# New places in the order of an attention and of the seam between two layers, with one small scratch moved out of PSUM

## The chip, the cores and the metric

The kernel runs on one core of a Trainium2 chip. Its time is the device time of one launch, in microseconds (us); lower is better. The engines are named as in the profile: PE (TensorE, matmuls; PEld is its weight load), DVE (VectorE), ACT (ScalarE), POOL (GpSimd) and SP, whose queue issues nearly all DMAs.

## What is computed

An attention over 2 x 8 heads (768 positions, 64 wide) in which a query sees only keys of the same hash bucket, and two layers behind it (1536 tokens, 512 wide, 2048 inside), cut here to its core:

```python
q_bits = (einsum('bhsd,dk->bhsk', q, proj) > 0)      # 6 bits give a bucket; k likewise
scores = where(q_bucket == k_bucket, q @ k.T / 8, -1e9)
x = softmax(scores) @ v                               # heads laid side by side: 1536 x 512
h = x @ w_in;  x = (P(h) / (Q(h) + 1e-6)) @ w_out     # layer 1, P cubic, Q with |h| and h*h
h = x @ w_in2; out = (h - tanh(h)) @ w_out2           # layer 2
```

## The kernel before

Heads go one after the other, h = 0 to 15, and each head in six steps j of 128 queries. A step multiplies scores into PSUM (`scores`, tiles st, L930), ACT takes the exponential (e, L933), ACT and DVE round it to 16 bits (eh, L942, L944), POOL takes the rest (el, L953), and PE multiplies both with V (`attend`, L985 to L988, with V's own high and low half in VB). Ahead of the scores of a head, six maxima are needed: PE makes the products a second time (`smax`, tiles sm, L810), DVE reduces each to a column of mx (L814), `put_max` turns the columns into rows with a transpose on PE (sbank<-ident,mx, L825), DVE negates them (mr, L831), and a DMA lays them into row 76 of TBq. The bucket bits come from `bits` on PE (L785), and DVE writes them into TBk (L795), from where a DMA takes 12 rows to TBq (L798). The operands of both products reach their places by DMAs within SBUF: `place` issues TBk and TBq (L768, L769), and `out_of place` four DMAs into TA (L775).

V is loaded for two heads at a time (`load_v`, tile vraw, L850). DVE takes the maximum of its magnitudes (vm, L854), a DMA lays the 128 pairs into one row (vrow, L859), the function `back` in `vall` reduces that row to two numbers and makes a power of two of each (L865 to L869), and a further DMA spreads them (vsc, L873). ACT then scales V into VB (L894), and `vmean_of` sums V on PE (sbank<-VB, L911), which ACT and DVE make into VM (L917, L918).

PSUM has three places for st, sm and bits tiles, which go round in the order in which the tiles are made, so that a new tile waits until the tile three before it was read. One further bank, sbank, is shared: the transposes of `put_max`, the sums of `vmean_of` and, on partition 64, the two numbers of `back` all lie in it, and the framework makes PE and DVE wait for each other there. `fill` puts matmuls without use on PE (pvw<-ones, L966).

All engines run in program order, and that order is written out by a list of tasks. Each task has a place on a line counted in steps of heads; the table MOVE shifts single tasks, and the tasks are emitted sorted by place:

```python
def on(place, fn, *args):
    tasks.append((place + MOVE.get(move_name(fn, args), 0), len(tasks), fn, args))
```

FILL lists places and counts of `fill`. After the attention a second list does the same with NUDGE, in microseconds of a plan. Between the layers, layer 2 works with sums and differences of blocks: `t_sum` (L1348) makes them on DVE, `x_hi` (ACT, L1359) and `x_lo` (DVE or POOL, L1365) split them, `product` multiplies (L1391), `u1`, `u2`, `u3` add products (`u2` is L1407), `g_lo` (POOL, L1470) gives the low half of the activation, and `y2_mm` (L1486) multiplies it.

Of the kernel before, what the change touches and what calls it, by code (L numbers as in the profile page):

```python
# [10 lines left out]
F32, F32R, F16, BF16, I32 = DT.float32, DT.float32r, DT.float16, DT.bfloat16, DT.int32  # L11
# [5 lines left out]
B, H, S, D = 2, 8, 768, 64  # L17
# [5 lines left out]
SH = S // 2  # L23
# [12 lines left out]
EH_ACT_LAST = (768, 0, 768, 384, 768, 768)  # L36
EL_DVE_LAST = (640, 0, 0, 384, 128, 768)

FILL = ((199.95, 71), (91.54, 25), (-29.26, 33), (-6.1, 72), (-0.79, 4), (-23.35, 19), (8.78, 3), (-23.45, 5), (1.45, 8))

VLO_POOL = (0, 1)

# [104 lines left out]
T_LAST = {'norm': 9.69, 'x': 10.12, 'x_out': 10.83}  # L147

NUDGE = {'stage_e 10 1': 1.68,
 't_sum 0 5 1 3': 1.0571,  # L150
 'rest2 2 1': -1.5624,
 'y_out 9 0': -0.62,
 't_sum 0 2 0 1': 2.09,
# [43 lines left out]
 'y2_mm 0 2': -1.047,  # L197
 'x_lo 1 6 1': -2.4416,
 'x_hi 1 6 1': -1.6436,
 'u3 1 1': 0.4716,  # L200
 'x_lo 0 3 1': 0.8634,
 'g_sub 0 a': 1.5846,
 'g_hi 0 a': 0.9366,
# [34 lines left out]
 'x_hi 0 6 0': 1.0934,  # L238
 'x_lo 0 6 0': 0.4954,
 'x_hi 0 5 1': 0.6058,  # L240
 'x_lo 0 5 1': 0.0078,
 'join2 3 1': -0.1334,
 'x_lo 0 4 0': 1.003,
 'g_lo 0 a': 0.3386,
# [5 lines left out]
 'x_hi 1 0 0': -0.2366,  # L250
 'g_lo 0 d': -1.1453,
 'g_hi 0 d': -0.6889,
 'g_sub 0 d': -0.0409}
MOVE = {'fill 25': 8.577,
 'attend 2 1': -0.953,
 'smax 15 0': -0.153,
# [14 lines left out]
 'vlo 10': 0.153,  # L271
 'smax 1 3': -0.091,
 'scale 1 1': -2.1579,
 'smax 0 2': -1.278,
 'out_of e (13, 2)': -0.263,
 'load_qk 2': 3.2764,
 'vall 0': 12.2053,
 'place 1': -0.1816,
 'round_e 8 5': 0.213,
 'out_of vmean 15': 0.073,  # L280
 'out_of place 1': 0.9139,
# [5 lines left out]
 'fill 19': -1.743,  # L287
 'out_of max (0, 2)': 0.006,
 'out_of max (13, 5)': 0.393,
 'load_qk 1': 0.1764,  # L290
 'attend 8 2': -0.953,
 'load_v 0': -1.2766,
 'attend 4 2': -0.953,
# [18 lines left out]
 'normalize 15': -0.377,  # L312
 'vhi 8': -0.1387,
 'attend 12 1': -0.883,
 'vhi 2': 0.553,
 'vlo 1': 0.073,
 'out_of place 3': -0.2893,
 'scores 13 0': 0.07,
 'round_e 15 5': 0.3926,
 'vmax 0': 10.6854,  # L320
 'scores 9 1': -0.055,
 'out_of max (0, 0)': 1.02,
 'smax 0 0': 1.318,
 'out_of bits 0': 10.916,
 'out_of e (15, 1)': -0.473,
 'scores 15 1': -0.055,
 'round_e 14 4': 0.006,
 'out_of e (14, 4)': -0.01,
 'load_v 1': 2.2916,
 'put_max 15': 0.633,  # L330
 'out_of put 15': 0.625,
 'out_of max (2, 5)': -0.7062,
 'smax 2 5': -0.4082,
 'out_of e (9, 2)': -0.263,
 'attend 13 0': -0.2423,
 'halves 0 1': 0.753,
# [7 lines left out]
 'out_of e (15, 0)': 0.8687,  # L344
 'round_e 15 0': 0.3407,
 'scale 0 1': 1.277,
 'out_of max (15, 4)': -1.2373,
 'smax 15 4': -0.9393,
 'scores 15 0': 0.948,
 'put_max 1': 0.203,  # L350
 'out_of put 1': 0.155,
# [7 lines left out]
 'out_of vmean 0': 0.403,  # L359
 'vhi 12': -0.023,  # L360
 'place 0': -0.568,
 'split_hi 0': -0.27,
 'smax 1 4': -0.153,
 'out_of e (13, 5)': -0.473,
 'scores 13 5': -0.055,
 'rest_e 15 4': 2.093,
 'vmean_of 1': 0.703,
 'out_of vmean 1': 0.553,
 'bits 0': 11.964,
 'smax 0 1': 0.024,  # L370
 'join 1 1': -1.01,
 'round_e 14 5': 1.0,
 'rest_e 14 5': 0.592,
 'attend 0 3': 0.193,
 'attend 14 1': -0.008,
 'scores 15 5': 0.413,
 'scores 7 0': 0.073,
 'round_e 0 2': 0.3044,
 'scale 3 1': -0.383,
 'attend 0 4': -0.103,  # L380
 'halves 2 0': 0.203,
 'scores 1 3': -0.093,
 'halves 2 1': 0.4539,
 'round_e 15 1': -0.003}
J0 = 2
YSQ = (0.9, 4, 3.5)
GC = dict(sub=0.7, hi=1.35, lo=1.95)
# [43 lines left out]
def tile_fn(ctx: ExitStack, tc: tile.TileContext, kq, v, proj, w1i, w1o, a_, b_, w2i, w2o, out):  # L431
# [236 lines left out]
    with ExitStack() as actx:  # L668
        actx.enter_context(tc.manual_schedule(engines={getattr(nc, e).engine for e in ORDERED}))
        ap = actx.enter_context(tc.tile_pool(name="ap", bufs=1))  # L670
# [4 lines left out]
        sbank = sgl.tile([P, 512], F32, name="sbank")  # L675
# [181 lines left out]
        def vall(pr):  # L857
            row = ap.tile([1, 2 * P], F32, name=f"vrow{pr}", tag="vrow", bufs=1)
            nc.sync.dma_start(row.rearrange("o (p h) -> o p h", h=2), vmx.pop(pr))  # L859
            sc = ap.tile([1, 2], F32, name=f"vs1{pr}", tag="vs1", bufs=2)  # L860

            def back():
                o = SH + D + 2 * (pr % 2)
                x = sbank[64:65, o:o + 2]
                nc.vector.tensor_reduce(x, row.rearrange("o (p h) -> o h p", h=2), axis=AX.X, op=ALU.max)  # L865
                xi = x.bitcast(I32)
                nc.vector.tensor_scalar(xi, xi, 0x7F800000, None, op0=ALU.bitwise_and)
                nc.vector.tensor_scalar(x, x, 2.0 ** -87, 2.0 ** -12, op0=ALU.max, op1=ALU.mult)
                nc.vector.reciprocal(sc, x)  # L869

            def again():
                vs = ap.tile([P, 2], F32, name=f"vsc{pr}", tag="vsc", bufs=3)
                nc.sync.dma_start(vs, sc.unsqueeze(1).to_broadcast([1, P, 2]))  # L873
                for j in range(2):
                    vsc[2 * pr + j] = vs[:, j:j + 1]

            outs["vback", pr], outs["vagain", pr] = back, again
# [161 lines left out]
        def on(place, fn, *args):  # L1039
            tasks.append((place + MOVE.get(move_name(fn, args), 0), len(tasks), fn, args))  # L1040
# [48 lines left out]
        for u in range(NE):  # L1089
            for fi in range(FG):  # L1090
                t = end + TT["h0"] + TT["slot"] * (4 * u + fi)
                on(t, h_mm, u, fi)
                for n, f in zip("abcde", (stage_a, stage_b, stage_c, stage_d, stage_e)):
                    on(t + TT[n], f, u, fi)
        for t, n in FILL:
            on(t, fill, n)
# [27 lines left out]
        for _, _, fn, args in sorted(tasks, key=lambda x: x[:2]):  # L1124
            name = fn.__name__
# [555 lines left out]
```

## Time and profile before

| | |
|---|---|
| median of 3 runs | 750.57 us (748.86 to 751.51) |
| profiled execution | 748.52 us, of which the span from first to last instruction is 746.8 us |
| busy in the span | PE 729.5 us (98%), DVE 616.5 (83%), ACT 551.8 (74%), POOL 538.4 (72%) |
| mean granted clock of TensorE | 0.993 of full speed |

Busy shares are means over stages. Since PE is busy for 98% of the span, what can be won without less work lies in the few places where PE waits and in stretches at the lower of its two clocks (0.5 in the profile is 1.2 GHz, 1.0 is 2.4 GHz). An interval in brackets in a timeline is the idle time of an engine ahead of that row, and the name behind the arrow is what ended it.

### The profile page before, as it was taken

To read this page: it belongs to the slowest core of one execution; us is meant where nothing else is said; L and a number is where in the kernel's file an instruction comes from. 1 tells how busy PE (TensorE), PEld (TensorE's weight loads), DVE (VectorE), ACT (ScalarE), POOL (GpSimd) and SP (SyncE) were. 2 spreads that over 40 slices of the span, in tenths; PEclk is the share of its full clock that TensorE was granted. 3 is DMA by queue.
4 is the path that set the end of the run, shared out by engine and by line. 5 is a ranking of instruction groups with operands and counts; after the bars stand their busy time and mean duration, and the time that the engine had idled before them with its cause. 6 is when DMAs were issued, how large, how long until landed. Compare 5 with 4: busy or idle time off the path is not lost.

```text
span 746.8 us, 14449 instructions
## 1 busy us (share of the span) xinstructions
PE 729.5 (98%) x5406; PEld 598.1 (80%) x5406; DVE 616.5 (83%) x1034; ACT 551.8 (74%) x979; POOL 538.4 (72%) x459
## 2 busy tenths in 40 slices
PE   8899999999999999999999999999999999999997
PEld 6788888888888888888888888887887676767664
DVE  7689998999968987899899999989666867778765
ACT  1688889988998787766776677688576768677652
POOL 2679898998998897777787789959646366364531
PEclk8999999999999999999999999999999999999999
DMA  7665546565420321212112212101030220311003
GB/s 197 170 163 141 151 115 173 163 150 166 124 86 30 113 85 57 70 61 69 56 57 86 75 39 70 44 2 56 29 114 32 83 85 29 113 57 57 29 29 140
DMA packets 43373, 66.56 MB, mean 89 GB/s; under 512 B 6164, under 2 KB 29812, under 8 KB 43304
## 3 DMA queue, kind: packets, MB, share of 16 engines
q1 hardware_dynamic: 43160, 65.52, 29.8%
q8 instruction: 42, 0.69, 0.4%
q14 instruction: 27, 0.22, 0.1%
q10 hardware_dynamic: 144, 0.13, 0.1%
HBM read 43.00 MB, written 3.15 MB: 62 GB/s over the span
## 4 chain that ended last, share of the span: by engine, by line
PE 74%; DVE 14%; ACT 4%; DMA 3%; POOL 2%; issue 2%; SPq 0%; POOLq 0%; ACTq 0%; DVEq 0%
PE y L1486 16%; PE h L609 16%; PE y L1179 16%; PE h2b L1391 6%; DVE mx L814 4%; PE st L930 4%; PE h2e L1391 4%; PE h2a L1391 4%; PE sm L810 2%; DVE TBk L795 1%; DVE eh L944 1%; POOL x L1365 1%; ACT e L933 1%; PE bits L785 1%; PE pv L985 1%
## 5 line engine op out<-in xcount | busy, mean ns | idle before, releaser
L953 POOL TENSOR_TENSOR el<-e,eh 128x768 f16<-128x768 f32 (+2 forms) x95 | 151.4, 1613 | 22.5 <-DVE eh L944 10.0
L1486 PE MATMUL y<-wS,g 128*128 128x512 f16 (+1 forms) x438 | 102.8, 378 | 0.0
L933 ACT ACTIVATE e<-st,lnk 128x768 f32<-128x768 f32 x96 | 86.1, 898 | 19.0 <-PE st L930 16.9
L814 DVE TENSOR_REDUCE mx<-sm 128x1 f32<-128x768 f32 x96 | 90.0, 950 | 9.5 <-PE sm L810 8.6
L1470 POOL TENSOR_TENSOR g<-tmp,g 128x384 f16<-128x384 f32 x48 | 44.0, 917 | 67.0 <-ACT g L1465 55.4
L665 POOL TENSOR_TENSOR G<-vec,G 128x512 fp32r<-128x512 f32 x44 | 57.2, 1306 | 26.0 <-ACT G L660 25.9
L1486 PEld LDWEIGHTS <-g 128*128 128x128 f16 x438 | 38.5, 98 | 45.6 <-issue 6.3
L1179 PE MATMUL y<-G,wO 128*128 128x512 f32 x288 | 67.1, 391 | 0.0
L1509 DVE SCALAR_TENSOR_TENSOR ya<-y,few,ya 128x512 f32<-128x512 f32 (+1 forms) x73 | 54.0, 741 | 15.0 <-PE y L1486 14.1
L1179 PE MATMUL y<-G,wE 128*128 128x512 f32 x288 | 66.3, 390 | 0.0
L609 PE MATMUL h<-x,wO 128*128 128x512 f32 x288 | 66.3, 390 | 0.0
L1179 PEld LDWEIGHTS y<-G,wE 128*128 128x128 f32 x288 | 54.1, 188 | 11.2
L609 PEld LDWEIGHTS h<-x,wO 128*128 128x128 f32 x288 | 54.1, 188 | 11.2
L1179 PEld LDWEIGHTS y<-G,wO 128*128 128x128 f32 x288 | 53.9, 188 | 11.3 <-POOL G L665 0.3
L942 ACT CAST eh<-e 128x384 f16<-128x384 f32 (+2 forms) x95 | 60.9, 642 | 1.7
L985 PEld LDWEIGHTS <-eh 128*128 128x128 f16 x576 | 53.1, 97 | 10.0 <-issue 9.9
L1391 PE MATMUL h2b<-x,wE 128*128 128x384 f32 x288 | 60.3, 344 | 0.8 <-ACT x L1359 0.8
L985 PE MATMUL pv<-VB,eh 128*128 128x65 f16 x540 | 57.8, 194 | 0.0
L988 PE MATMUL pv<-VB,el 128*128 128x65 f16 x540 | 57.0, 192 | 0.8 <-POOL el L953 0.8
L986 PE MATMUL pv<-VB,eh 128*128 128x64 f16 x540 | 57.4, 195 | 0.0
L930 PE MATMUL st<-TA 128*128 128x384 f32 x192 | 56.4, 375 | 0.5 <-DVE mx L814 0.3
L810 PE MATMUL sm<-TBk,TBq 76*128 76x384 f32 x192 | 52.2, 357 | 3.2 <-DVE TBq L792 2.1
(202 smaller groups left out, 2039.0 us busy)
## 6 DMA issues: line engine op xcount, KB each, us to landing
raw<-in_w1i_dram SPq DMA_DIRECT2D x16, 512.0 KB
raw<-in_w1o_dram SPq DMA_DIRECT2D x16, 512.0 KB
raw<-in_w2i_dram SPq DMA_DIRECT2D x16, 512.0 KB
raw<-in_w2o_dram SPq DMA_DIRECT2D x16, 512.0 KB
kq<-in_kq_dram SPq DMA_DIRECT2D x16, 384.0 KB
TA<-A SPq DMA_DIRECT2D x32, 192.0 KB
TA<-Bl SPq DMA_DIRECT2D x32, 192.0 KB
vraw<-in_v_dram SPq DMA_DIRECT2D x8, 384.0 KB
```

The costliest lines, as they stand in the source:

```text
L609: nc.tensor.matmul(ps, l[:, dc], r, start=(n == 0), stop=(n == 11))
L810: nc.tensor.matmul(ps[:, n], TBq[h][0:76, j * P:(j + 1) * P], TBk[h][0:76, n * SH:(n + 1) * SH], start=True, stop=True)
L814: d = nc.vector.tensor_reduce(mx[h][:, j:j + 1], ps, axis=AX.XY, op=ALU.max)
L930: nc.tensor.matmul(ps[:, n], l[h][0:k, j * P:(j + 1) * P], q[h][0:k, n * SH:(n + 1) * SH], start=(k == P), stop=(k < P))
L933: outs["e", (h, j)] = lambda: nc.scalar.activation(halved(e), ps, AF.Exp, scale=1.0 / math.sqrt(D), bias=lnk)
L942: nc.scalar.copy(t[:, 0:r], e[:, 0:r])
L953: nc.gpsimd.tensor_sub(l[:, r:NK], e[:, r:NK], eh[h, j][:, r:NK])
L985: nc.tensor.matmul(out(t), a[:, t], vb[:, j, 0:PW], start=False, stop=False, skip_group_check=True)
L986: nc.tensor.matmul(out(t)[:, 0:D], a[:, t], vb[:, j, PW:PW + D], start=False, stop=False, skip_group_check=True)
L1179: nc.tensor.matmul(ps, l[:, o], r, start=(n == 0), stop=(n == 11))
L1391: nc.tensor.matmul(banks[n, k], w_in(j, l)[:, o:o + P], x[:, r, dt], start=new and z == 0, stop=z == 5, skip_group_check=not new)
L1486: nc.tensor.matmul(ps[:, c], g[:, l, o], r[:, c], start=(z == 0), stop=(z == 5))
```

## The change

One function changes: the two numbers in `back` lie in a tile of their own in SBUF (vx, two buffers) and no longer in sbank. Everything else is numbers of three tables: FILL, MOVE (about 50 entries changed or added) and NUDGE (4). Where a shift is small it changes nothing; the core of what the diff says is:

```diff
-FILL = ((199.95, 71), (91.54, 25), (-29.26, 33), (-6.1, 72), (-0.79, 4), (-23.35, 19), (8.78, 3), (-23.45, 5), (1.45, 8))
+FILL = ((199.95, 71), (91.54, 25), (-29.26, 52), (-6.1, 72), (-23.35, 19), (6.47, 1), (-11.01, 3))
...
- 't_sum 0 5 1 3': 1.0571,
+ 't_sum 0 5 1 3': -1.4768,
...
- 'load_qk 1': 0.1764,
+ 'load_qk 1': -1.4262,
...
- 'load_v 1': 2.2916,
+ 'load_v 1': 2.2339,
...
             def back():
-                o = SH + D + 2 * (pr % 2)
-                x = sbank[64:65, o:o + 2]
+                x = ap.tile([1, 2], F32, name=f"vx{pr}", tag="vx", bufs=2)
                 nc.vector.tensor_reduce(x, row.rearrange("o (p h) -> o h p", h=2), axis=AX.X, op=ALU.max)
                 xi = x.bitcast(I32)
                 nc.vector.tensor_scalar(xi, xi, 0x7F800000, None, op0=ALU.bitwise_and)
```

The fill counts in the order of the program: 57 become 71 at the start; 3 come new between the maxima of head 0; 76 become 72 ahead of st of head 0, step 0; 8 behind its step 1 go; 3 behind the scores of head 1, step 2 become 1 ahead of those of step 1.

SP's queue at the opening. Names are tiles with running numbers; kq is the load of a head's K and Q, A the rounded K and Q of a head. Before:

```order
L713 DMA kq_109<-in_kq_dram 128x768
L719 DMA praw_108<-in_proj_dram 128x6
L850 DMA vraw_186<-in_v_dram 128x6x128
L768 DMA TBk_192<-A_188 64x768
L769 DMA TBq_193<-A_188 64x768
L713 DMA kq_196<-in_kq_dram 128x768
L775 DMA TA_191<-A_188 64x768 x2
L775 DMA TA_191<-Bl_189 64x768 x2
L768 DMA TBk_232<-A_218 64x768
L769 DMA TBq_233<-A_218 64x768
L859 DMA vrow_259<-vm_236 1x128x2
L713 DMA kq_272<-in_kq_dram 128x768
```

After the change:

```order
L739 DMA kq_109<-in_kq_dram 128x768
L745 DMA praw_108<-in_proj_dram 128x6
L876 DMA vraw_205<-in_v_dram 128x6x128
L739 DMA kq_207<-in_kq_dram 128x768
L794 DMA TBk_214<-A_209 64x768
L795 DMA TBq_215<-A_209 64x768
L801 DMA TA_213<-A_209 64x768 x2
L801 DMA TA_213<-Bl_210 64x768 x2
L739 DMA kq_268<-in_kq_dram 128x768
L885 DMA vrow_270<-vm_245 1x128x2
L794 DMA TBk_279<-A_237 64x768
L795 DMA TBq_280<-A_237 64x768
```

The load of head 1 stands ahead of the first `place`, and the load of head 2 and the small row vrow stand ahead of the second `place`.

SP's queue some 20 us later, around the load of the second piece of V (vraw, for heads 2 and 3). Before:

```order
L713 DMA kq_385<-in_kq_dram 128x768
L768 DMA TBk_388<-A_373 64x768
L769 DMA TBq_389<-A_373 64x768
L775 DMA TA_387<-A_373 64x768 x2
L775 DMA TA_387<-Bl_374 64x768 x2
L798 DMA TBq_389<-TBk_388 12x768
L850 DMA vraw_447<-in_v_dram 128x6x128
L713 DMA kq_463<-in_kq_dram 128x768
L768 DMA TBk_517<-A_486 64x768
L769 DMA TBq_518<-A_486 64x768
```

After the change:

```order
L739 DMA kq_403<-in_kq_dram 128x768
L794 DMA TBk_406<-A_391 64x768
L795 DMA TBq_407<-A_391 64x768
L876 DMA vraw_455<-in_v_dram 128x6x128
L801 DMA TA_405<-A_391 64x768 x2
L801 DMA TA_405<-Bl_392 64x768 x2
L824 DMA TBq_407<-TBk_406 12x768
L794 DMA TBk_473<-A_465 64x768
L795 DMA TBq_474<-A_465 64x768
L739 DMA kq_477<-in_kq_dram 128x768
```

The load of V stands five DMAs earlier (four into TA and the 12 rows of bits), and the load of head 4 two later.

PE around the transposes and the sum of V of head 1 (st are scores of head 0, sm products for the maxima of head 2). Before:

```order
L810 MATMUL sm_0_557<-TBk_388,TBq_389 128x384 x2
L930 MATMUL st_4_569<-TA_191 128x384 x2
L930 MATMUL st_4_569<-TBq_193,TBk_192 128x384 x2
L825 MATMUL sbank<-ident,mx_407 6x128
L810 MATMUL sm_1_582<-TBk_388,TBq_389 128x384 x2
L911 LDWEIGHTS ones_84
L911 MATMUL sbank<-VB_137,ones_84 128x64
```

After the change:

```order
L955 MATMUL st_4_563<-TA_213 128x384 x2
L955 MATMUL st_4_563<-TBq_215,TBk_214 128x384 x2
L836 MATMUL sm_0_569<-TBk_406,TBq_407 128x384 x2
L851 MATMUL sbank<-ident,mx_417 6x128
L955 MATMUL st_5_589<-TA_213 128x384 x2
L955 MATMUL st_5_589<-TBq_215,TBk_214 128x384 x2
L836 MATMUL sm_1_594<-TBk_406,TBq_407 128x384 x2
L936 LDWEIGHTS ones_84
L936 MATMUL sbank<-VB_137,ones_84 128x64
```

The scores of step 5 stand ahead of the sum of V and no longer behind it, and the product for the first maximum of head 2 stands behind the scores of step 4.

On ACT and POOL, rounding head 3's K and Q (A, Bl) stands one step earlier. Elsewhere in the attention single tasks change places: st of heads 7 and 8, step 0, stand one `attend` later, the sum of V of head 7 stands behind the next scores, and `put_max` of head 15 one `attend` earlier. Between the layers, one `t_sum` stands three rows earlier on DVE, and `u2` of the first block now stands between two `x_lo` instead of behind both; ACT and POOL keep their order there.

## Rows read from the trace of the kernel before

**Rows 1.** Timeline of PE, 24 to 36 us: start, us, engine, line, operation, [idle before, releaser].

```profile
24.42 0.52 PE L930 MATMUL st<-TA 128*128 128x384 f32 x2
...
25.13 0.60 PE L966 MATMUL pvw<-ones 128*128 128x122 f16 x8
25.63 1.26 PE L810 MATMUL sm<-TBk,TBq 76*128 76x384 f32 x4
...
34.80 0.80 PE L911 MATMUL sbank<-VB,ones 128*128 128x64 f16 x12 [2.31 <-DVE mr L831]
35.41 0.99 PE L930 MATMUL st<-TA 128*128 128x384 f32 x2
```

**Rows 2.** Timeline of DVE in the same stretch, same columns.

```profile
24.62 0.96 DVE L814 TENSOR_REDUCE mx<-sm 128x1 f32<-128x768 f32 x1
...
30.56 0.95 DVE L814 TENSOR_REDUCE mx<-sm 128x1 f32<-128x768 f32 x1
33.60 0.95 DVE L854 TENSOR_REDUCE vm<-vraw 128x2 f32<-128x768 f32 x1 [2.10 <-DMA vraw<-in_v_dram]
...
38.56 0.96 DVE L814 TENSOR_REDUCE mx<-sm 128x1 f32<-128x768 f32 x1 [0.19 <-PE sm L810]
...
41.96 0.96 DVE L814 TENSOR_REDUCE mx<-sm 128x1 f32<-128x768 f32 x1 [1.27 <-PE sm L810]
```

**Rows 3.** Timeline of the SP queue, 22 to 28 us: one row a piece of DMA issues.

```profile
22.13 1.25 SPq L775 DMA_DIRECT2D TA<-A  x2
...
26.73 0.79 SPq L798 DMA_DIRECT2D TBq<-TBk  x1
27.55 0.50 SPq L850 DMA_DIRECT2D vraw<-in_v_dram  x1
```

**Rows 4.** Stretches: length, busy us of PE, PEld, DVE, ACT, POOL, granted clock, DMA share.

```profile
33.00:34.60 1.60, 0.00 (x0) 0.00 (x0) 1.00 (x2) 0.53 (x2) 1.60 (x2) 1.00 0.07 21
34.60:38.00 3.40, 3.20 (x35) 2.89 (x34) 3.24 (x7) 1.08 (x3) 1.60 (x2) 0.50 0.29 58
...
10.70:17.50 6.80, 6.77 (x35) 5.28 (x35) 5.76 (x12) 0.83 (x1) 1.81 (x1) 0.50 0.78 198
```

**Rows 5.** Waits of PE over the span: who waited for whom, us, times, longest.

```profile
PE sbank L825 <- DVE vs L869: 1.8, 3, 0.8
```

**Rows 6.** Timeline of DVE, 55 to 58 us: last maximum and end of the scratch chain.

```profile
55.92 0.95 DVE L814 TENSOR_REDUCE mx<-sm 128x1 f32<-128x768 f32 x1
...
57.77 0.17 DVE L869 RECIPROCAL vs<-sbank 1x2 f32<-1x2 f32 x1
```

**Rows 7.** Timeline of PE at 133 us: one of the three waits of rows 5.

```profile
133.77 0.27 PE L825 MATMUL sbank<-ident,mx 128*6 128x128 f32 x1 [0.56 <-DVE vs L869]
```

**Rows 8.** Chain that ended last, 133 to 135 us: start, us, what.

```profile
133.03 1.83 POOL Bl L760
```

**Rows 9.** Chain that ended last, at 159 us.

```profile
159.22 0.27 PE sbank L825
```

**Rows 10.** Timeline of PE, opening.

```profile
1.08 4.53 PE L966 MATMUL pvw<-ones 128*128 128x122 f16 x57 [1.08 <-DVE q1c L598]
...
8.80 1.32 PE L810 MATMUL sm<-TBk,TBq 76*128 76x384 f32 x6 [2.06 <-DVE TBq L792]
...
21.97 0.59 PE L810 MATMUL sm<-TBk,TBq 76*128 76x384 f32 x2 [0.35 <-DMA TBq<-TBk]
```

**Rows 11.** Timeline of ACT, opening: the wait before V is scaled.

```profile
21.50 0.62 ACT L894 ACTIVATE VB<-vraw,vsc 128x384 f16<-128x384 f32 x1 [2.12 <-DMA vsc<-vs]
```

**Rows 12.** Timeline of PE between the two layers.

```profile
499.93 1.30 PE L1391 MATMUL h2b<-x,wE 128*128 128x384 f32 x6 [0.76 <-ACT x L1359]
...
509.39 2.09 PE L1486 MATMUL y<-wO,G 128*128 128x512 f32 x8 [1.15 <-POOL G L1470]
```

**Rows 13.** Timeline of DVE between the layers.

```profile
499.24 0.55 DVE L1407 TENSOR_TENSOR tmp<-h2b,tmp 128x384 f32<-128x384 f32 x1
```

**Rows 14.** Timeline of POOL between the layers.

```profile
507.04 2.30 POOL L1470 TENSOR_TENSOR G<-tmp,G 128x384 fp32r<-128x384 f32 x2
```

More of the change, by code (lines that the diff above doesn't have):

```diff
@@ L199 @@
  'x_hi 1 6 1': -1.6436,
- 'u3 1 1': 0.4716,
+ 'u3 1 1': -0.845,
  'x_lo 0 3 1': 0.8634,
@@ L240 @@
  'x_hi 0 5 1': 0.6058,
- 'x_lo 0 5 1': 0.0078,
+ 'x_lo 0 5 1': 0.0138,
  'join2 3 1': -0.1334,
@@ L252 @@
  'g_hi 0 d': -0.6889,
- 'g_sub 0 d': -0.0409}
+ 'g_sub 0 d': -0.0409,
+ 'y2_out 2 2': 0.6828}
 MOVE = {'fill 25': 8.577,
@@ L273 @@
  'scale 1 1': -2.1579,
- 'smax 0 2': -1.278,
+ 'smax 0 2': -1.243,
  'out_of e (13, 2)': -0.263,
- 'load_qk 2': 3.2764,
+ 'load_qk 2': -0.8365,
  'vall 0': 12.2053,
- 'place 1': -0.1816,
+ 'place 1': 12.6501,
  'round_e 8 5': 0.213,
@@ L314 @@
  'attend 12 1': -0.883,
- 'vhi 2': 0.553,
+ 'vhi 2': 1.023,
  'vlo 1': 0.073,
@@ L319 @@
  'round_e 15 5': 0.3926,
- 'vmax 0': 10.6854,
+ 'vmax 0': 11.55,
  'scores 9 1': -0.055,
- 'out_of max (0, 0)': 1.02,
- 'smax 0 0': 1.318,
- 'out_of bits 0': 10.916,
+ 'out_of max (0, 0)': 1.061,
+ 'smax 0 0': 1.355,
+ 'out_of bits 0': 10.953,
  'out_of e (15, 1)': -0.473,
@@ L328 @@
  'out_of e (14, 4)': -0.01,
- 'load_v 1': 2.2916,
[L330 to L333, printed above, removed]
+ 'load_v 1': 2.2339,
+ 'put_max 15': -0.2439,
+ 'out_of put 15': -0.2519,
+ 'out_of max (2, 5)': -1.1504,
+ 'smax 2 5': -0.8524,
  'out_of e (9, 2)': -0.263,
@@ L346 @@
  'scale 0 1': 1.277,
- 'out_of max (15, 4)': -1.2373,
- 'smax 15 4': -0.9393,
+ 'out_of max (15, 4)': -1.423,
+ 'smax 15 4': -1.125,
  'scores 15 0': 0.948,
@@ L361 @@
  'place 0': -0.568,
- 'split_hi 0': -0.27,
+ 'split_hi 0': -1.3028,
  'smax 1 4': -0.153,
@@ L368 @@
  'out_of vmean 1': 0.553,
- 'bits 0': 11.964,
- 'smax 0 1': 0.024,
+ 'bits 0': 12.001,
+ 'smax 0 1': 0.059,
  'join 1 1': -1.01,
@@ L373 @@
  'rest_e 14 5': 0.592,
- 'attend 0 3': 0.193,
+ 'attend 0 3': 0.187,
  'attend 14 1': -0.008,
@@ L378 @@
  'round_e 0 2': 0.3044,
- 'scale 3 1': -0.383,
+ 'scale 3 1': -0.377,
  'attend 0 4': -0.103,
  'halves 2 0': 0.203,
- 'scores 1 3': -0.093,
+ 'scores 1 3': -0.087,
  'halves 2 1': 0.4539,
- 'round_e 15 1': -0.003}
+ 'round_e 15 1': -0.003,
+ 'smax 8 4': 0.883,
+ 'vmean_of 2': 0.433,
+ 'split_lo 0': -2.4888,
+ 'out_of max (2, 2)': -0.703,
+ 'smax 2 2': -0.405,
+ 'round_e 1 4': 0.143,
+ 'scores 6 4': -0.433,
+ 'scores 0 4': -0.444,
+ 'put_max 2': 0.006,
+ 'out_of max (8, 4)': 0.585,
+ 'attend 6 1': -0.883,
+ 'vlo 15': -1.807,
+ 'out_of place 2': 4.8369,
+ 'round_e 1 1': 0.473,
+ 'rest_e 1 1': 0.065,
+ 'place 3': -0.893,
+ 'split_hi 3': -1.0739,
+ 'split_lo 3': -1.0569,
+ 'smax 15 5': 0.923,
+ 'out_of max (15, 5)': 0.625,
+ 'attend 7 1': -0.953,
+ 'scores 0 5': -0.25,
+ 'rest_e 14 2': 1.212,
+ 'rest_e 14 3': 0.215,
+ 'round_e 7 0': 0.008}
 J0 = 2
```

## The prediction

> **What bounds the kernel now.** I read the waits of PE first, because PE is busy nearly throughout and only its idle places and its slow stretches leave anything to win. Then I followed each place on the timelines of PE, DVE, ACT, POOL and SP, and last on the chain that ended last, to see whether the recovered time would reach the end.
>
> The dearest place is 32 to 38 us. The sum of V of head 1 on PE starts at 34.80 after 2.31 us of idleness, and its releaser is mr on DVE [rows 1]. But DVE itself was not busy: it had taken the last maximum of head 1 at 30.56, done at 31.51, and then stood 2.10 us before vm until the load of vraw had landed at 33.60 [rows 2]. mr is queued behind vm. That load was issued at 27.55 [rows 3], so it took 6.05 us from issue to use. The stall has a second price: the granted clock was 1.00 while PE idled from 33.0 to 34.6, and 0.50 (1.2 GHz) in the 3.40 us that follow, in which PE was busy for 3.20 us [rows 4]. A pair of score matmuls took 0.99 us there against 0.52 us at 24.42 [rows 1]. DVE felt that too: it waited 0.19 and 1.27 us for sm, the second time until 41.96 [rows 2].
>
> The second kind of place is the shared bank. Three times PE held its transposes of the maxima until the last operation of `back` was done, 1.8 us in all [rows 5]; one of the three is 0.56 us at 133.77 [rows 7], the longest 0.8. The third kind lies in the opening [rows 10, 11], the fourth between the layers [rows 12].
>
> **The change, part by part.**
>
> *The load of V, and the order of PE behind it.* The load moves five issues ahead, to where the issues into TA began at 22.13, so 5.4 us earlier [rows 3]. Even with the same 6.05 us to landing it is there at 28.2, 3.3 us before DVE asks for it at 31.51. So the 2.10 us go. The transposes still wait for the last maximum, but behind them PE now has the scores of step 5 and one sm, some 1.2 us of work at the pace of rows 1, while DVE does vm (0.95) and mr. What is late next is vm itself, which still lies ahead of mr; I leave 0.15 us of wait there. The size of the gain has two measures. On DVE the waits from 31.51 to 41.96 add up to 2.10 + 0.19 + 1.27 = 3.56 us. On PE it is 2.31 plus what the low clock cost, at most half of 3.20 busy us = 1.60, together 3.9. The smaller one binds, as DVE must do its work in order: 3.56 - 0.15 = 3.4 us. Bounds: 2.1 if the clock falls somewhere else all the same, 3.9 if DVE does not bind.
>
> The Trainium skill (TensorE: Matmul & The Clock Gate, section Terms) prices a slow stretch as its time times the share of clock lost, which for the 3.40 us of rows 4 is an estimate of 1.7 us. By it the place would give 2.31 + 1.7 = 4.0 us and the whole sum 742.9 instead of 743.5 us. The trace agrees with the rule (1.60 against 1.7), but the DVE rows, not PE's, set my term.
>
> *The scratch.* The two numbers in SBUF do not share a bank with PE, so its transposes wait for the last maximum only. At 57 us that one ends at 55.92 + 0.95 = 56.87, the scratch chain at 57.94 [rows 6]: 1.07 us earlier, more than the longest of the three waits, so all 1.8 us leave PE. Do they reach the end? At 159 us the chain runs straight into those transposes [rows 9], and the wait there, 0.8 us, counts; the one at 57 us (1.8 - 0.8 - 0.56 = 0.45) too, as PE is released there by the scratch alone. At 133 us the chain runs on POOL [rows 8], and PE's 0.56 us are hidden behind it. Together 1.25 us; bounds 0.45 (one place) and 1.8. The four operations themselves cost the same wherever the numbers lie, as near as rows tell: DVE has the whole chain from 56.87 to 57.94 in 1.07 us for two numbers, and I found no reason for a shorter or a longer one beyond a tenth.
>
> *The opening.* Here the signs differ. The 14 more fills take 14 x 4.53/57 = 1.1 us at the rate of the first row of rows 10, and 14 x 0.60/8 = 1.05 at that of rows 1; they stand ahead of the first `bits`, from which DVE's chain and sm at 8.80 hang, and the 2.06 us of idleness ahead of sm is DVE's work, which stays. Cost: up to 1.1 us. On the other side SP now issues the loads of heads 1 and 2 and vrow ahead of the `place` DMAs, so that A of head 1, the scratch chain and the spreading of vsc come sooner; ACT stood 2.12 us for vsc [rows 11] and PE 0.35 us for the bits of head 1 [rows 10]. Gain: up to 2.12, of which the later start takes its 1.1. Bounds -0.75 (the delay less the 0.35 us of wait that it hides) and +1.0; I take +0.35, the wait at 21.97, somewhat above the middle, because the earlier issues reach that wait directly.
>
> *Fills.* The 8 that go stood 0.50 us ahead of sm at 25.63, but this sm could not start before DVE had read the tile three places before, at 24.62 + 0.96 = 25.58 [rows 1, 2]. They filled a wait and cost nothing; 0, bounds 0 and 0.5.
>
> *Between the layers.* The idle 0.76 us before 499.93 are put down to ACT, but DVE's u2 ends at 499.24 + 0.55 = 499.79, right before it [rows 12, 13], and u2 now stands one `x_lo` (0.6 us) earlier. That takes some 0.6 us from this wait. But the next one, until 509.39, is for POOL, which was still at the first two low halves from 507.04 to 509.34 [rows 12, 14] and keeps its order; what PE wins before, it waits there longer. 0, bounds 0 and 0.6. The other moved tasks of heads 7 to 15 swap neighbours on PE; I put them at 0 with a bound of 0.7 either way.
>
> Sum: 3.4 + 1.25 + 0.35 = 5.0 us, so 748.52 - 5.0 = 743.5 for the profiled execution. That execution lies 2.05 us under the median of 750.57; the sum against the median gives 745.6, against the mean of all four known times (749.87) 744.9. I take 745.3.
>
> **The rivals.**
>
> *More: the opening keeps its clock.* From 10.7 to 17.5 us the clock was 0.50 too [rows 4]. If the additional fills hold it at 1.00, PE's work in these 6.8 us shrinks, and the opening gives its +1.0 and, of the 6.77/2 = 3.4 us that PE gets back, perhaps half, since DVE's own work there stays. For it: fills stand on both sides of the stretch. Against it: the 2.06 us of idleness ahead of 8.80 remain. 5.0 + 0.65 + 1.7 = 7.35, so 743.2.
>
> *Less: the queue.* With V's load ahead, the issue at 26.73, the 12 rows of bits for head 2, comes behind a whole load more. If it takes the 6.05 us that the load of V took, it lands at 32.8, and PE has the first sm of head 2 ahead of the transposes, which could start at 31.5; PE then stalls 1.3 us and may pay up to 1.6 us of low clock as before. 5.0 - 1.3 - 1.6 = 2.1 us are left, about 748.5. Against it: four issues into TA stood right ahead of that issue before as well, the first at 22.13 [rows 3].
>
> *Nothing: another engine takes over.* Behind 42 us DVE and POOL have little room; the chain's POOL piece at 133.03 [rows 8] shows that PE is not always the bound. If the whole attention runs at their pace, the time won at 32 us is waited off later: 749.6 to 751.6. Against it: DVE's waits at 38 and 41 us were waits for PE.
>
> *Slower: the first operands come late.* The load of head 1 now lies ahead of TBk and TBq of head 0, which sm at 8.80 needs. If the loads of V and of head 1 in front and the operands themselves each take the 6.05 us of the load above [rows 2, 3], they land 18.2 us into the span, and sm starts 9.4 us late: 750.57 - 5.0 + 9.4 = 755.0. It decides from a start of sm later than 16.1 (8.80 + 5.0 + 2.25). Against it: what that load waited for were the DMAs issued just ahead of it, and in the opening little is ahead. The Trainium skill (DMA: Bandwidth & Descriptors, section Queues, rings and completion order) says that each DMA engine takes its descriptors in ring order, which is the mechanism of this rival and of the queue above. No row here shows the order inside the queue.
>
> **How the numbers follow.** The forecast, 3.3 to 6.8 us won: 0.66. More: 0.10. Queue, 1 to 3.3 us: 0.13, half of it on each side of 2.25. Nothing: 0.06. Slower: 0.05. A measurement tells 0.3%, 2.25 us, from no change. Faster 0.66 + 0.10 + 0.07 = 0.83, same 0.06 + 0.06 = 0.12, slower 0.05. The forecast's own times are 743.8 to 747.3; the range 742.4 to 748.4 adds nearly all of More and half of the queue's case, so about 0.8.
>
> **What would show it.** Right: no wait of DVE for vraw near 31 us; sum of V of head 1 within 0.3 us of PE's last sm; clock 1.00 from 20 us on; maximum 3 of head 2 some 3.9 us earlier than 41.96; no PE wait for vs; the wait for POOL between the layers grown by what the one before lost. Wrong: sm of head 0 later than 10; PE waiting for TBq's bits of head 2 near 31 us; the gain at 42 us gone by the end of the attention.

## The result and the profile after

The changed kernel takes 757.24 us (median of 6 runs, 754.45 to 758.97) against 749.19 us (6 runs, 748.51 to 751.51) before: ratio 1.0095, with 95% interval 1.0077 to 1.0113. It is slower by some 7 us, where 5 us of gain were forecast. The profiled execution took 754.45 us, with a span of 752.6 us.

Up to 54 us the forecast came true. The timelines of DVE (30 to 39 us) and then of PE (31 to 34 us) answer to [rows 1] and [rows 2]:

```profile
30.68 0.95 DVE L840 TENSOR_REDUCE mx<-sm 128x1 f32<-128x768 f32 x1
31.54 0.94 DVE L880 TENSOR_REDUCE vm<-vraw 128x2 f32<-128x768 f32 x1
32.72 0.28 DVE L857 TENSOR_SCALAR mr<-sbank 6x128 fp32r<-6x128 f32 x1 [0.24 <-PE sbank L851]
...
38.70 0.96 DVE L840 TENSOR_REDUCE mx<-sm 128x1 f32<-128x768 f32 x1
...
31.98 0.59 PE L836 MATMUL sm<-TBk,TBq 76*128 76x384 f32 x2 [0.21 <-DMA TBk<-A]
...
33.22 0.51 PE L836 MATMUL sm<-TBk,TBq 76*128 76x384 f32 x2
33.57 0.55 PE L936 MATMUL sbank<-VB,ones 128*128 128x64 f16 x12
```

DVE takes vm right behind the last maximum, where it had stood 2.10 us. PE's sum of V follows its sm without a gap, where it had idled 2.31 us. The maximum that had stood at 41.96 us now stands at 38.70 us. At the transposes of the maxima of head 3 PE is 4.0 us ahead (the changed kernel, then the kernel before):

```profile
53.98 0.27 PE L851 MATMUL sbank<-ident,mx 128*6 128x128 f32 x1
...
57.99 0.27 PE L825 MATMUL sbank<-ident,mx 128*6 128x128 f32 x1 [0.48 <-DVE vs L869]
```

Then the lead is lost. The next rows are the waits of PE from 50 to 190 us (who waited for whom, us, times, longest):

```profile
PE sbank L936 <- DVE mr L857: 3.8, 4, 1.1
PE sbank L851 <- DVE mx L840: 2.6, 1, 2.6
PE st L955 <- DVE mx L840: 1.6, 3, 1.0
```

The waits for the last operation of `back` [rows 5] are gone, as predicted. In their place PE waits for maxima and for mr, so DVE is late. The groups of DVE by form show why. The first two rows are of the changed kernel, the last two of the kernel before (count, busy us, mean ns, idle):

```profile
L893 DVE TENSOR_SCALAR vx<-vx 1x2 f32<-1x2 f32 x8 | 10.6, 1325 | 0.3
...
L892 DVE TENSOR_SCALAR vx<-vx 1x2 int32<-1x2 int32 x8 | 2.5, 316 | 0.3
```

```profile
L867 DVE TENSOR_SCALAR sbank<-sbank 1x2 int32<-1x2 int32 x8 | 1.4, 172 | 0.3
L868 DVE TENSOR_SCALAR sbank<-sbank 1x2 f32<-1x2 f32 x8 | 1.4, 172 | 0.3
```

Two operations on two numbers each had cost 2.8 us over the span, and now cost 13.1 us. That is 10.3 of the 10.7 us by which DVE's busy time grew (616.5 to 627.2 us). The timelines of DVE, POOL and PE around one of them:

```profile
53.77 0.16 DVE L892 TENSOR_SCALAR vx<-vx 1x2 int32<-1x2 int32 x1
53.96 1.72 DVE L893 TENSOR_SCALAR vx<-vx 1x2 f32<-1x2 f32 x1
55.71 0.15 DVE L894 RECIPROCAL vs<-vx 1x2 f32<-1x2 f32 x1
55.80 0.93 DVE L840 TENSOR_REDUCE mx<-sm 128x1 f32<-128x768 f32 x1
56.65 0.27 DVE L857 TENSOR_SCALAR mr<-sbank 6x128 fp32r<-6x128 f32 x1
...
53.83 1.83 POOL L786 TENSOR_TENSOR Bl<-kq,A 128x768 fp32r<-128x768 f32 x1
55.62 1.63 POOL L978 TENSOR_TENSOR el<-e,eh 128x768 f16<-128x768 f32 x1
...
56.97 0.53 PE L936 MATMUL sbank<-VB,ones 128*128 128x64 f16 x12 [1.10 <-DVE mr L857]
```

POOL begins Bl at 53.83 us and is done at 55.66. DVE's operation begins at 53.96 and is done at 55.68, 0.02 us behind it. mr and the last maximum come 1.6 us late, and PE pays 1.10 us. The profile counts the time in which DVE stands as busy, so no wait shows on DVE. One must read the mean duration of a group of tiny operations to see it. In the chain that begins at 36.58 us, with POOL idle beside it, both operations took 0.16 us. The chain that ended last, followed from 183 to 190 us (start, us, what), shows the dearest place:

```profile
183.89 1.44 DVE vx L892
...
185.35 1.74 DVE vx L893
...
187.12 0.15 DVE vs L894
187.28 0.86 DVE mx L840
...
188.18 0.27 PE sbank L851
```

Both are stuck there, PE idles 2.60 us, and the clock is low behind it (stretches, columns as in [rows 4]):

```profile
185.00:189.00 4.00, 1.40 (x24) 1.28 (x21) 3.93 (x6) 1.40 (x3) 3.67 (x3) 1.00 0.15 48
189.10:192.50 3.40, 3.40 (x37) 3.09 (x36) 3.27 (x7) 1.73 (x2) 2.61 (x2) 0.50 0.18 39
```

The opening (to [rows 10]) and the seam between the layers (to [rows 12]) on PE:

```profile
1.09 5.70 PE L991 MATMUL pvw<-ones 128*128 128x122 f16 x71 [1.09 <-DVE q1c L624]
...
10.48 1.32 PE L836 MATMUL sm<-TBk,TBq 76*128 76x384 f32 x6 [2.60 <-DMA TBq<-A]
...
22.33 0.51 PE L836 MATMUL sm<-TBk,TBq 76*128 76x384 f32 x2
...
504.48 1.28 PE L1416 MATMUL h2b<-x,wE 128*128 128x384 f32 x6 [0.28 <-DVE tmp L1432]
...
507.18 1.31 PE L1416 MATMUL h2b<-x,wE 128*128 128x384 f32 x6 [0.38 <-ACT x L1384]
...
514.87 2.11 PE L1511 MATMUL y<-wO,G 128*128 128x512 f32 x8 [0.89 <-POOL G L1495]
```

### The profile page after: what moved, and what is told of

Read it like the earlier page. It is cut to its first block, busy times and chain, and to the rows that moved or that the text cites. A ratio compares the mean times of both kernels' runs of the same rounds, so it can differ in the third digit from the quotient of the medians.

```text
span 752.6 us, 14451 instructions
## 1 busy us (share of the span) xinstructions
PE 732.7 (97%) x5409; PEld 597.9 (79%) x5409; DVE 627.2 (83%) x1034; ACT 552.2 (73%) x979; POOL 539.1 (72%) x459
## 4 chain that ended last, share of the span: by engine, by line
PE 66%; DVE 19%; POOL 5%; ACT 4%; issue 3%; DMA 3%; SPq 1%; ACTq 0%; DVEq 0%; POOLq 0%
PE y L1511 16%; PE h L635 12%; PE y L1204 12%; PE h2b L1416 6%; DVE mx L840 5%; PE st L955 4%; PE h2e L1416 4%; PE h2a L1416 4%; PE sm L836 2%; DVE eh L969 1%; DVE vx L893 1%; PE bits L811 1%; DMA kq<-in_kq_dram 1%; POOL G L691 1%; POOL wE L1335 1%
```

## The experiments

Each was timed against the kernel before on the same chip. The kernels named in the first four blocks were compared together, and so were the next four, the four after them, and the last two.

**bank_back**: the changed kernel, scratch in sbank again.

```diff
-                x = ap.tile([1, 2], F32, name=f"vx{pr}", tag="vx", bufs=2)
+                o = SH + D + 2 * (pr % 2)
+                x = sbank[64:65, o:o + 2]
```

> The changed kernel with the two numbers of v's maximum back in TensorE's bank, every new place kept. Port theory: the two scalar operations on the two numbers take 172 ns each again instead of 316 and 1325 ns, DVE is busy some 10 us less, the lead of 4.0 us that PE has at 54 us lasts to the end of the attention except for the waits at the bank that come back (1.25 us by the prediction), and between the layers it loses about 1 us as the changed kernel does: 746.5 us, between 745 and 748.5. Rival, the new places are to blame: the lead is lost between 54 and 240 us all the same and it takes 754 us or more.

Measured: 747.99 us, ratio 0.9983 (0.9972 to 0.9995). The new places do not lose the time: with the scratch in the bank they gain 1.3 us. On numbers in PSUM both scalar operations always took 172 or 173 ns (durations min/median/max in ns, first and last start in us), although in all 16 cases POOL was at work beside them:

```profile
L893 DVE TENSOR_SCALAR sbank<-sbank x8: 172/172/173, 17.8 to 178.6; 1x2 int32<-1x2 int32 x8
L894 DVE TENSOR_SCALAR sbank<-sbank x8: 172/172/173, 18.0 to 178.8; 1x2 f32<-1x2 f32 x8
```

**sbuf_only**: the kernel before with the opposite edit.

> The kernel before with nothing changed but the scratch, now in SBUF. Port theory: in heads 2 to 15 one of the two scalar operations stands until the POOL operation beside it ends, DVE is busy 5 to 11 us longer, and the time is 753 to 758 us (749.2 plus 4 to 9). Rival, the scratch is harmless and the places are to blame: 747 to 749.5 us, the gain that the prediction gave it or nothing.

Measured: 764.45 us, ratio 1.0183 (1.0160 to 1.0206). The scratch alone costs 13.7 us, more than either theory said. In PE's waits from 50 to 200 us, mr counts for 7.4 us in 5 places and a maximum for 2.6 us in one, where the kernel before had 0.7 us for mr and 1.8 us for the bank.

**one_col**: the changed kernel, two operations on one number each in place of one on two.

```diff
-                nc.vector.tensor_scalar(xi, xi, 0x7F800000, None, op0=ALU.bitwise_and)
-                nc.vector.tensor_scalar(x, x, 2.0 ** -87, 2.0 ** -12, op0=ALU.max, op1=ALU.mult)
+                for j in range(2):
+                    nc.vector.tensor_scalar(xi[:, j:j + 1], xi[:, j:j + 1], 0x7F800000, None, op0=ALU.bitwise_and)
+                for j in range(2):
+                    nc.vector.tensor_scalar(x[:, j:j + 1], x[:, j:j + 1], 2.0 ** -87, 2.0 ** -12, op0=ALU.max, op1=ALU.mult)
```

> The changed kernel, scratch in SBUF, but each of the two scalar operations is made as two operations on one number each, so there are no two halves to read side by side. Port theory in its narrow form (an operation takes the second port, and waits for POOL, only where it has two numbers to share out): four operations of some 156 ns, none stuck, about 0.3 us more DVE work per pair of heads; 744 to 747.5 us. Rival (any DVE scalar operation from SBUF to SBUF waits for POOL, or the numbers are slow to come back from SBUF): one of the four is stuck 1.5 us in heads 2 to 15 as now; 756 to 759 us.

Measured: 744.13 us, ratio 0.9927 (0.9913 to 0.9941): faster than both kernels. Of the tile's operations (columns as above) none is stuck any more, though POOL was at work beside 28 of the 32 single ones; the last two rows, of DVE and of POOL, show a pair of them inside POOL's Bl:

```profile
L893 DVE TENSOR_SCALAR vx<-vx x16: 130/136/142, 17.7 to 176.9; 1x1 int32<-1x1 int32 x16
L895 DVE TENSOR_SCALAR vx<-vx x16: 130/137/143, 17.8 to 177.1; 1x1 f32<-1x1 f32 x16
L890 DVE TENSOR_REDUCE vx<-vrow x8: 396/398/406, 17.2 to 176.4; 1x2 f32<-1x256 f32 x8
...
53.70 0.20 DVE L895 TENSOR_SCALAR vx<-vx 1x1 f32<-1x1 f32 x2
...
53.56 1.84 POOL L786 TENSOR_TENSOR Bl<-kq,A 128x768 fp32r<-128x768 f32 x1
```

**nudge_only**: the kernel before with the four changed numbers of NUDGE alone.

> The kernel before with the new places between the layers alone. Prediction's step: the wait of 0.75 us ahead of 499.93 gets some 0.6 us shorter and the wait for POOL ahead of 509.39 as much longer, 749.2 us within 0.5. Rival: these places cost the 1.0 to 1.5 us that the changed kernel loses between 485 and 515 us, 750.2 us or more.

Measured: 749.55 us, ratio 1.0004 (0.9990 to 1.0018). The places between the layers are worth nothing that these runs can tell.

**onecol_before**: the kernel before with the scratch in SBUF and single operations (the edits of sbuf_only and one_col).

> The kernel before with the scratch in SBUF, its scalar operations on one number at a time, and no other change: the second step of the prediction by itself. The step as predicted: PE's three waits at the bank go and 1.25 us reach the end (0.45 to 1.8), so 748.5 us. Rival: the shared bank cost more than those three waits, since the changed kernel with the scratch in the bank and with single operations in SBUF stood 3.9 us apart; then 745.5 to 746.5.

Measured: 748.30 us, ratio 0.9982 (0.9970 to 0.9995), 1.3 us. That is the second step's predicted size, though not its working (see below). The rival's 3.9 us are the distance in the new order (747.99 against 744.13); in the old order it is smaller.

**onecol_late_v**: one_col, with V's load issued behind the 12 rows of bits of head 2.

```diff
- 'load_v 1': 2.2339,
+ 'load_v 1': 2.45,
```

> The changed kernel with single operations in SBUF (744.1 us), with the load of V of heads 2 and 3 issued where it was before, behind the 12 rows of bits of head 2: the first step of the prediction by itself. The step as predicted: DVE stands some 2 us for vraw again, PE behind it, the clock falls to 0.50 for some 3 us, and the time rises by 3.4 us (2.1 to 3.9) to 747.5. Rival: PE's new order (step 5's scores ahead of the sum of V) hides most of the wait, and the time rises by less than 1.5 us.

Measured: 745.44 us, ratio 0.9950 (0.9937 to 0.9963), so 1.7 us more than one_col by the ratios, between the two theories. DVE did stand 2.0 us and PE 1.4 us, but the clock did not fall. In the stretch of the stall:

```profile
34.00:38.00 4.00, 2.59 (x53) 2.21 (x54) 3.22 (x6) 1.89 (x4) 1.86 (x2) 1.00 0.44 130
```

The stretch in [rows 4] stood at 0.50. Half of the step as predicted was therefore not there to be lost.

**onecol_loads_back**: one_col, with the loads of heads 1 and 2 back behind the operands.

```diff
- 'load_qk 1': -1.4262,
- 'load_qk 2': -0.8365,
+ 'load_qk 1': 0.1764,
+ 'load_qk 2': 3.2764,
```

> The changed kernel with single operations in SBUF (744.1 us), with the loads of heads 1 and 2 behind the operands of heads 0 and 1 again (the row of maxima behind TA of head 0). The prediction's step: the earlier loads saved PE and ACT waits in the opening, 1.1 to 2.1 us by the rows, so without them 745 to 746. Rival, the prediction's slower case in small: the load of head 1 holds up TBk and TBq of head 0, sm of head 0 starts near 9 instead of 10.05, and the time falls to 743 or below.

Measured: 743.86 us, ratio 0.9927 (0.9915 to 0.9940), the same as one_col. Neither theory: sm of head 0 began as late as in one_col, and the time did not move.

**step2**: the changed kernel, two numbers in each operation, not side by side.

```diff
-                x = ap.tile([1, 2], F32, name=f"vx{pr}", tag="vx", bufs=2)
+                x = ap.tile([1, 4], F32, name=f"vx{pr}", tag="vx", bufs=2)[:, 0:3:2]
```

> The changed kernel, scratch in SBUF, two numbers in each scalar operation, but with a gap of one number between them. If an operation takes the second port whenever it has two numbers to share out, it is stuck beside POOL as in the changed kernel: 755 to 759 us. If the two must lie side by side for that, nothing is stuck and it takes what single operations take: 743 to 745 us.

Measured: 756.18 us, ratio 1.0092 (1.0077 to 1.0106). The float operation's median is 1707 ns. A gap between the two numbers does not help.

**onecol_early_v**: onecol_before, with V's load ahead of the four issues into TA, nothing else.

```diff
- 'load_v 1': 2.2916,
+ 'load_v 1': 2.2339, 'out_of place 2': 4.8369,
```

> The kernel before with single operations in SBUF (748.3 us), and of the new places only the load of V of heads 2 and 3, ahead of the four issues into TA as in the changed kernel; the order of the other engines is that of before. If the early load is what removes the stall, the low clock at 34.6 us goes with it and it takes 3.4 us less (2.1 to 3.9): 744.9 us. Rival: half of the gain belongs to PE's new order, as the late load cost the changed kernel's order only 1.6 us; then 746.5 us or more.

Measured: 746.61 us, ratio 0.9960 (0.9947 to 0.9973), 1.6 us less than onecol_before. The rival is right: the early load is worth some 1.6 us, in either order of PE. PE's waits that are left between 20 and 45 us:

```profile
22.27 0.59 PE L810 MATMUL sm<-TBk,TBq 76*128 76x384 f32 x2 [0.60 <-DMA TBq<-TBk]
...
24.23 0.51 PE L912 MATMUL sbank<-VB,ones 128*128 128x64 f16 x11 [0.28 <-POOL VB L902]
...
31.90 0.58 PE L810 MATMUL sm<-TBk,TBq 76*128 76x384 f32 x2 [0.45 <-DMA TBq<-TBk]
...
42.74 0.62 PE L931 MATMUL st<-TA 128*128 128x384 f32 x2 [0.78 <-ACT e L934]
```

**out_of_place**: the changed kernel, two numbers, the result in another tile than the source.

```diff
-                nc.vector.tensor_scalar(x, x, 2.0 ** -87, 2.0 ** -12, op0=ALU.max, op1=ALU.mult)
+                z = ap.tile([1, 2], F32, name=f"vz{pr}", tag="vz", bufs=2)
+                nc.vector.tensor_scalar(z, y, 2.0 ** -87, 2.0 ** -12, op0=ALU.max, op1=ALU.mult)
```

The integer operation writes to y in the same way.

> The changed kernel, two numbers in each scalar operation in SBUF, but each operation writes to another tile than it reads. If an operation with two numbers from SBUF to SBUF takes the second port, it is stuck beside POOL as in the changed kernel: 755 to 759 us. Rival, it is stuck for being in place: 743 to 746 us.

Measured: 756.31 us, ratio 1.0089 (1.0063 to 1.0115). Working in place is not the cause.

**onecol_nonudge** and **onecol_fills**: one_col with NUDGE, or with FILL, of the kernel before.

> The changed kernel with single operations in SBUF (744.0 us) and the places between the layers of before. The prediction's step: what the first wait there loses, the later ones gain, so 744.0 within 0.7. Rival: the new places cost the about 1 us that PE loses between 490 and 515 us: 743.0.

> The changed kernel with single operations in SBUF (744.0 us) and the fills of before: 14 fewer at the start, 8 more behind step 1 of head 0, none of the others. The prediction's steps: the 14 stand ahead of work that waits anyway or cost up to 1.1 us, the 8 fill a wait: 743 to 744.5 us. Rival: without them PE idles longer in the opening and the clock is low for longer or again: 745.5 us or more.

Measured: 743.77 us and 743.75 us, ratios 0.9917 (0.9898 to 0.9935) and 0.9917 (0.9898 to 0.9937). Neither table makes a difference that these runs can tell.

**bl_halves**: the changed kernel, POOL's Bl cut in two.

```diff
-            (nc.gpsimd if h else nc.vector).tensor_sub(lo, raw.pop(h), hi)
+            r = raw.pop(h)
+            if h == 0:
+                nc.vector.tensor_sub(lo, r, hi)
+            else:
+                for n in range(2):
+                    c = slice(n * SH, (n + 1) * SH)
+                    nc.gpsimd.tensor_sub(lo[:, c], r[:, c], hi[:, c])
```

> The changed kernel, scratch in SBUF with two numbers in each operation, but POOL makes the low half of the next head's kq in two operations of half the width. If the scalar operation stands for POOL's running operation, it is now let go when a half ends: its median falls from 1.7 us to about 0.9 us or less, each of the six or seven stuck operations ends within 0.05 us of the end of a half, and the time falls from 757.2 by 3 to 6 us to 751 to 754. Rival, it stands for something else that takes 1.7 us: median unchanged, 756 to 758.

Measured: 751.67 us, ratio 1.0020 (1.0001 to 1.0040). The tile's view, first the integer operation and then the float one:

```profile
L898 DVE TENSOR_SCALAR vx<-vx x8: 156/157/1436, 18.5 to 183.0; 1x2 int32<-1x2 int32 x8
L899 DVE TENSOR_SCALAR vx<-vx x8: 156/886/931, 18.7 to 184.4; 1x2 f32<-1x2 f32 x8
```

The median fell from some 1.7 us to 0.89 us because an operation on another engine was cut in two: it is POOL's running operation for which DVE stands. DVE's own work was left alone, and 5.6 us came back.

**onecol_heads0to3**: onecol_before with the changed kernel's entries of MOVE for heads 0 to 3 (31 entries); those of heads 6 to 15, FILL and NUDGE stay as before.

> The kernel before with single operations in SBUF and the changed kernel's places for heads 0 to 3, those of heads 6 to 15, the fills and the layers as before. If the remaining 2.6 us come from the opening's rows (PE idled 0.4 us at 31.5 and 0.8 at 42 without them, and not with them), 744.0 to 745 us. Rival, they come from heads 6 to 15: 746 us or more.

Measured: 743.78 us, ratio 0.9927 (0.9900 to 0.9954), the whole gain of one_col. The moved rows of heads 6 to 15 are worth nothing that these runs can tell; the interval is some 4 us wide. None of the four waits of onecol_early_v stands in its trace.

## Why the prediction was wrong

**The step that failed** is the last sentence on the scratch: "The four operations themselves cost the same wherever the numbers lie, as near as rows tell". They do not. In SBUF, a `tensor_scalar` on two numbers that starts while POOL is inside an operation stands until POOL's ends: all 40 that took over 0.3 us, in five kernels, end 17 to 25 ns behind an operation of POOL. The row it was read from, 1.07 us for the whole chain [rows 6], was of numbers in PSUM, and no row of the kernel before had two numbers in SBUF beside POOL. By the ratios, the changed kernel against one_col, the stuck operations cost 1.0095 - 0.9927 = 0.0168, or 12.6 us, and turned a gain of 5.5 us into a loss of 7. None of the rivals had this mechanism. Two of the prediction's three signs of being wrong came in full, sm of head 0 later than 10 us and a gain that is gone by the end of the attention; only the second belongs to this step. The rival that ended slower had the wrong place: sm of head 0 did start at 10.48 us, but PE had made that up at 22.33 us, within 0.4 us of [rows 10].

The Trainium skill (SBUF — State Buffer, section Who interferes with whom) states this mechanism: `tensor_scalar` from SBUF to SBUF can run in a mode that uses a second pair of ports, which GpSimd also uses, and of the two the later one blocks for the whole operation of the other. The trace agrees: the stuck operations end 0.02 us behind POOL's, two numbers get stuck, one does not, and with numbers in PSUM neither does. The page speaks against this change and was not weighed.

**The other steps**, measured with one_col's operations in place of the stuck ones:

- *V's load and the order behind it, 3.4 us, with the opening's 0.35 us.* The rows of heads 0 to 3 gave 0.9982 - 0.9927 = 0.0055, 4.1 us (give or take 2 us, by the intervals), so the size fits. Its working was not. The early load by itself gives 1.6 us. The low clock at 34.6 us, which made up some 1.5 us of the step, stood in the one execution that was read and in no other with a trace: in four further executions with the late load (nudge_only, onecol_before, onecol_late_v, sbuf_only), DVE's wait for vraw was 1.8, 0.3 and 2.0 us and none, and the clock of this place was 1.00 in all four. The agreement of 1.60 with 1.7 us in the prediction compares two workings of that one stretch and shows nothing more. The remaining 2.5 us come from other moved rows of heads 0 to 3, of which the step had only used PE's new order behind the stall, as cover for vm; the loads of heads 1 and 2 and the fills have no part in them. The traces show where: onecol_heads0to3 is 2.55 us ahead of onecol_early_v at the transposes of head 2 (table below), and the four waits that it lacks are 2.1 us of that. Which row removes which wait was not tried.
- *The scratch's wait at the bank, 1.25 us*: 1.3 us by the ratio, once the operations are not stuck, but partly by luck. By the table below, one execution of each kernel, the bank costs 2.4 us from head 2 to head 15 in the old order and 2.2 us in the new. The wait at 133 us, which the step had called hidden, reaches head 15 too: the lead of onecol_before over nudge_only grows there from 1.25 to 1.97 us. At the start of layer 1 a wait that the step did not have takes about half of that back: PE's first product there waits for an operation of DVE. It does so in onecol_before and in bank_back (the two rows), and not in nudge_only, one_col or the kernel before, although DVE and PE have the same operations in the same order up to there.

```profile
PE h L609 <- DVE wt L510: 1.2, 1, 1.2
...
PE h L635 <- DVE wt L536: 1.1, 1, 1.1
```

Starts on PE in us, from the traces: the transposes of the maxima of head 2 and of head 15, and the first product of layer 1 (h).

| kernel | head 2 | head 15 | layer 1 |
|---|---|---|---|
| nudge_only (old order, bank) | 45.89 | 209.70 | 242.89 |
| onecol_before (old order, SBUF) | 45.28 | 206.72 | 241.16 |
| bank_back (new order, bank) | 42.54 | 204.72 | 240.75 |
| one_col (new order, SBUF) | 42.66 | 202.69 | 237.53 |
| onecol_early_v | 44.82 | 206.46 | 240.91 |
| onecol_heads0to3 | 42.27 | 203.75 | 238.18 |

- *The opening's earlier loads*: nothing, as the ratios with and without them are equal. The fills did not lift the clock there either: from 10 to 20 us its mean is 0.66 before and after, so the rival of a faster opening falls.
- *Fills and layers at 0*: right. Between the layers three waits of 0.28, 0.38 and 0.89 us stand where 0.76 and 1.15 us had stood [rows 12].
- *The later heads at 0*: right.
- *The queue's rival* was there in small: in the changed kernel sm of head 2 waited 0.21 us for its operands at 31.98 us, and with the early load alone 0.45 us for the 12 rows of bits at 31.90 us.

Added up by ratios, the steps without the failed sentence come to 0.9927, some 5.5 us, against the 5.0 us predicted. The sum is near, but two of its terms have their size for other reasons than the prediction gave.

What stays open: which moved rows of heads 0 to 3 remove the four waits, and why the place of two numbers decides whether PE's first product of layer 1 waits for DVE. That wait, of 1.1 to 1.2 us, comes in the new order with the scratch in the bank and in the old order with the scratch in SBUF; by the table that is most of the difference between 3.9 and 1.3 us.

## What to carry to other kernels

Where a `tensor_scalar` on DVE gets its operands in SBUF in place of PSUM, ask what POOL does beside it, since one that takes 0.16 us for two numbers can stand behind an operation of POOL until it has taken 1.73 us, and the profile counts that as DVE busy. A mean far above the minimum in a group of tiny operations, with ends that fall together with POOL's, is the sign. Before a gain is built on a stall and a slow stretch of one execution, ask which of the two must recur: of four further executions two had the stall in full, none the low clock.

## What was not expected of the hardware

One number instead of two is enough: 32 operations on one number took 130 to 143 ns each, 28 of them with POOL at work beside them, so four small operations were cheaper than two. The reduction from SBUF to SBUF (396 to 406 ns) and the reciprocal on two numbers (152 to 154 ns) were never stuck. Nor were DVE's casts to eh of 128x384, from SBUF to SBUF, which have a mean of 550 ns in both kernels although POOL was at work beside 21 of the 31. Why these run freely was not tried. The shift of weights (`low`, a `tensor_scalar` on 128x512 integers) kept a mean of 685 ns in both; it writes to PSUM, as the chain in the bank does.
